# Decode attention with a parallel MLP: V in 4 MB transfers of 32 heads, P turned by VectorE, the last rows of w4 behind V

## The chip, the core and the metric

The kernel runs on one core of a Trainium2 chip. The metric is device microseconds of one execution. Before the change the median of three runs is 215.27 us (215.07 to 215.28). Engines are named TensorE (PE in the profile, PEld for its weight loads), VectorE (DVE), ScalarE (ACT), GpSimd (POOL) and SyncE (SP), which issues nearly all transfers.

## The reference

```python
x = A_x                                   # 4 x 1 x 576, bf16
xn = _layernorm(x)
return x + _A_ref(xn, k_cache, v_cache, wq, wo) + _B_ref(xn, w1, w2, w3, w4)

def _A_ref(...):                          # B = 4, 32 query heads, 16 K/V heads, head size 128
    q = x @ wq                            # one position per batch
    k, v = the last W = 2048 rows of each cache of 8192 rows, each K/V head for two query heads
    p = softmax(q k^T * 128 ** -0.5)
    return (p v) @ wo                     # wo: 4096 x 576

def _B_ref(...):                          # 576 -> 576 -> 4608 -> 576
    h = gelu(layernorm(x) @ w1)
    g0..g3 = the four quarters of h, each shifted along the sequence (which has length 1)
    x1 = x + concat(g0..g3) @ w2
    return x1 + gelu(layernorm(x1) @ w3) @ w4
```

K and V of the window are 33.6 MB each in bf16; the weights are some 21 MB. Everything is read from HBM once.

## The kernel before

The work is one stream of transfers and, beside it, four engines' instruction lists. `add(engine, emit, waits, sig, key)` files an instruction under an engine; each list is sorted by `key` and emitted in that order, with a semaphore wait for each name in `waits`. A list is strictly in order: an instruction that waits holds up all behind it. SyncE's list holds the transfers: wq, w1, w2, w3, w4 in two parts (24 rows and 12 rows per partition), sixteen of K, sixteen of V, five of wo.

**K.** Chunk `c` of K is one batch and four heads (`CH`), 2 MB: partition p holds 64 rows of 128 values, 16 KB in one piece (`kv_src`). There are four slots (`kslot`); K4 and later wait until TensorE has turned the chunk that held the slot (`T`, L496). VectorE and ScalarE copy the turned blocks (L480, L479), and TensorE multiplies them with the padded queries into scores that stay in PSUM (L503).

**Softmax and P.** After the last scores VectorE takes the maximum (L509), ScalarE the exponentials (L513). P has to be turned so that keys lie on partitions. For that VectorE makes four masked copies of each quarter (`dve_mask`, L521), TensorE gathers them by 16 products (`pe_PT`, L530), ScalarE copies, TensorE applies a permutation (L541), ScalarE copies again (L543).

**V.** V comes in the same 2 MB chunks into five slots (`vslot`), the sixteenth into a slot of K. V0 to V4 wait until w4 has been used (`MO1`), V5 and later for the product of the chunk five before (`PV`). For a chunk VectorE spreads P over 32 columns per group of four rows (`dve_pad`, L559: 512 elements per partition); TensorE makes 16 products of 32 columns of P by 512 columns of V, four side by side in column tiles (L567); VectorE masks the useful blocks and sums them (L585, L588); TensorE folds partitions (L573); VectorE scales (L591). Fifteen chunks run in a hardware loop of three turns of five, the last outside it, with idle products ahead of it and of the last fold (`IDLE`).

**The end.** The result is turned (L601 to L603, `ORT`) and multiplied with wo's 32 rows per partition (L386), which come in pieces of 12, 10, 7, 2 and 1 rows (`WO_ROWS`) into three of K's slots once K has been turned. The MLP's sum, kept in `t1f`, is added to the same accumulator (`pe_t1f`, L610). Two copies and two small transfers end the program.

Of the kernel before, what the change touches and what calls it, by code (L numbers as in the profile page):

```python
# [12 lines left out]
NKT = 16  # L13
# [3 lines left out]
NVS = 5  # L17
ACT_EVAC = (1, 4, 7)
WO_ROWS = (12, 10, 7, 2, 1)
IDLE = {NKT - 2: 5, NKT - 1: 5}  # L20
# [14 lines left out]
def bass_parallel_sum__sliding_block_cached__mixer_s_mlp__decode_kernel(  # L35
# [23 lines left out]
    CH = [(b, gq) for gq in range(4) for b in range(B)]  # L59
    x2 = A_x.rearrange("b s d -> (b s) d")  # L60
# [3 lines left out]
    with ExitStack() as ctx:  # L64
# [12 lines left out]
        vslot = lambda c: vring[:, c % NVS * UE:(c % NVS + 1) * UE] if c < NC - 1 else kslot(0)  # L77
# [6 lines left out]
        w4t = vring[:, 4 * F:4 * F + W4R * D].rearrange("p (r n) -> p r n", r=W4R)  # L84
        assert 4 * F + W4R * D <= 5 * UE
        wot = kring[:, UE:UE + 32 * D].rearrange("p (r n) -> p r n", r=32)
        assert 32 * D <= 3 * UE
# [13 lines left out]
        P4 = cut(4 * NU * 512).rearrange("p (q t u i) -> p q t u i", q=4, t=16, u=NU)  # L101
        PTx = cut(4 * 512).rearrange("p (q x) -> p q x", q=4)
        PTpad = cut(NVS * NT * 2 * NU).rearrange("p (s t u e) -> p s t u e", s=NVS, t=NT, u=NU)
        tmp = [cut(2 * 512).bitcast(FP32).rearrange("p (t d) -> p t d", t=4) for _ in range(2)]
        assert _o <= NKT * 1024
        PTv = PT_t[:].rearrange("p (t c e) -> p t c e", t=NT, c=NC)

        acc = sb("acc", [128, NVS, 128], FP32)
# [16 lines left out]
        q_sb = acc[:].rearrange("p a b -> p (a b)").bitcast(BF16)[:, 0:1024].rearrange("p (k x) -> p k x", k=2)  # L125
# [5 lines left out]
        permT_bf = sb("permT_bf", [128, 128], BF16)  # L131
        ident_f = sb("ident_f", [128, 128], FP32)
        ones_f = sb("ones_f", [128, 128], FP32)
        mask4 = sb("mask4", [128, NU], FP32)
        maskd = sb("maskd", [128, 4], FP32)
        sel_f = sb("sel_f", [128, 32], FP32)
        sel_bf = sb("sel_bf", [128, 32], BF16)
        sel8 = sb("sel8", [128, 2 * NU], FP32)
        mU = sb("mU", [128, NU], FP32)
        mU_bf = sb("mU_bf", [128, NU, 2], BF16)  # L140
# [19 lines left out]
        PTps = [ps[:, 4 + k, :].rearrange("p (t x) -> p t x", t=16) for k in range(4)]  # L160
        OTps = [ps[:, 4, 8 * k:8 * k + 8] for k in range(NVS)]
        PVb = [0, 1, 2, 3, 6]
        rinvps = ps[:, 5, 0:128]
        ORps = ps[:, 6, 0:128]
# [18 lines left out]
        for k in range(NVS):  # L183
            for nm in ("PD", "FF", "AA", "OO"):
                S[nm, k] = sem(f"{nm}{k}")
# [31 lines left out]
        for c in range(NC):  # L217
            k, i = c % NVS, c // NVS
            ev_val[f"PV{c}"] = ("PV", c + 1)
            ev_val[f"fold{c}"] = ("FO", c + 2)  # L220
            ev_val[f"pad{c}"] = (("PD", k), i + 1)
            ev_val[f"F{c}"] = (("FF", k), i + 2)
            ev_val[f"A{c}"] = (("AA", k), i + 1 + (k == NVS - 1))
            ev_val[f"O{c}"] = (("OO", k), i + 1 + (k >= NVS - 2))
# [25 lines left out]
        P(lambda e: e.memset(acc[:, NVS - 1, :], 0.0), key=-88, inc=(("AA", NVS - 1), 1))  # L250
        for nm, k in [("FF", k) for k in range(NVS)] + [("OO", NVS - 2), ("OO", NVS - 1)]:
            P(lambda e, nm=nm, k=k: e.sem_inc(S[nm, k], 1), key=-87)


        def mask_of(t, tag, view, axis=AX.X):
            add("dve", lambda e: e.tensor_reduce(out=t[:], in_=view, axis=axis, op=ALU.add), waits=["ident_f"], sig=tag, key=-8)
        mask_of(mask4, "mask4", ident_f[:].rearrange("p (u x) -> p u x", u=NU))
        mask_of(maskd, "maskd", ident_f[:].rearrange("p (j t y) -> p t j y", j=4, t=4), AX.XY)
        mask_of(sel_f, "sel_f", ident_f[:].rearrange("p (u x) -> p x u", u=NU))
        mask_of(sel8, "sel8", ident_f[:].rearrange("p (k x) -> p x k", x=2 * NU))  # L260
        add("dve", lambda e: e.tensor_copy(out=sel_bf[:], in_=sel_f[:]), waits=["sel_f"], sig="sel_bf", key=-7.9)
        mask_of(mU, "mU", ident_f[:].rearrange("p (i u) -> p u i", u=NU))
        for x in range(2):
            add("dve", lambda e, x=x: e.tensor_copy(out=mU_bf[:, :, x], in_=mU[:]), waits=["mU"], sig=f"mU_bf{x}", key=-7.8)
# [10 lines left out]
        ev_w4 = [add_dma([(w4t[:, W4P[k]:W4P[k + 1], :], w4s[:, W4P[k]:W4P[k + 1], :])], ("w4", k), (), -45 + k)  # L275
# [5 lines left out]

        t_done = lambda c: f"T{NBLK * c + NBLK - 1}"
        ev_v = []
# [3 lines left out]
        for c in range(NC):  # L287
# [174 lines left out]
        def pe_MO(k):  # L462
            def f(e):
                ins = None
                for t in range(W4P[k], W4P[k + 1]):
                    for h in range(2):
                        ins = acc_mm(e, h, h2T_sb[:, t, :], w4t[:, t, HALF * h:HALF * (h + 1)], stop=(t == W4R - 1))
                return ins
            return f
        for k in range(2):  # L470
            add("pe", pe_MO(k), waits=[ev_w4[k], "h2T", "t1acc"], sig=f"MO{k}", key=-10 + k)
        add("dve", lambda e: e.tensor_copy(out=t1f[0:B, :], in_=ACC[0]), waits=["MO1"], sig="t1f0", key=-4)
        add("act", lambda e: e.activation(out=t1f[32:32 + B, :], in_=ACC[1], func=ACTF.Copy), waits=["MO1"], sig="t1f1", key=-4)
# [43 lines left out]
        def dve_mask(q):  # L517
            def f(e):
                ins = None
                for u in range(NU):  # L520
                    ins = e.tensor_scalar(out=P4[:, q, :, u, :], in0=P_sb[:, q, :].rearrange("p (t i) -> p t i", t=16),  # L521
                                          scalar1=mask4[:, u:u + 1], scalar2=None, op0=ALU.mult)
                return ins
            return f

        def pe_PT(q):
            def f(e):
                ins = None
                for t in range(16):
                    ins = e.matmul(PTps[q][:, t, :], lhsT=P4[:, q, t].rearrange("p u i -> p (u i)"), rhs=sel_bf[:],  # L530
                                   start=True, stop=True, skip_group_check=True)
                return ins
            return f
        for q in range(4):
            k0 = KS + 0.2 + 0.1 * q
            add("dve", dve_mask(q), waits=[f"exp{q}", "mask4"], sig=f"P4_{q}", key=k0)
            add("pe2", pe_PT(q), waits=[f"P4_{q}"] + (["sel_bf"] + [f"E{NB - 1 - k}" for k in range(4)] if q == 0 else []),
                sig=f"PTp{q}", key=k0)
            add("act", lambda e, q=q: e.activation(out=PTx[:, q, :], in_=ps[:, 4 + q, :], func=ACTF.Copy),  # L539
                waits=[f"PTp{q}"], sig=f"PTx{q}", key=k0 + 0.05)  # L540
            add("pe2", lambda e, q=q: e.matmul(ps[:, q, :], lhsT=permT_bf[:], rhs=PTx[:, q, :], start=True, stop=True),  # L541
                waits=[f"PTx{q}", "permT_bf"], sig=f"PTy{q}", key=k0 + 0.11)
            add("act", lambda e, q=q: e.activation(out=PT_t[:, 512 * q:512 * (q + 1)], in_=ps[:, q, :], func=ACTF.Copy),  # L543
                waits=[f"PTy{q}"], sig=f"PT{q}", key=k0 + 0.16)
# [5 lines left out]
            waits=["diag", "ones_f", "PT3"], sig="rinvp", key=KV + 0.5)  # L550
        add("dve", lambda e: e.tensor_copy(out=rinvB[:].rearrange("p (c u e) -> p c u e", u=NU, e=2),
                                           in_=rinvps.rearrange("p (u c e) -> p c u e", u=NU, e=2)),
            waits=["rinvp"], sig="rinvB", key=KV + 1.5)


        def dve_pad(c):
            b, gq = CH[c]
            cc = 4 * b + gq
            return lambda e: e.tensor_tensor(out=PTpad[:, c % NVS],  # L559
                                             in0=PTv[:, :, cc, :].unsqueeze(2).to_broadcast([128, NT, NU, 2]),  # L560
                                             in1=mU_bf[:].unsqueeze(1).to_broadcast([128, NT, NU, 2]), op=ALU.mult)

        def emit_PV(e, k, v):
            ins = None
            for g in range(NT // 4):
                j = g % 4
# [8 lines left out]
        def pe_idle(n):  # L575
            def f(e):
                for _ in range(n):
                    e.matmul(ps[:, 5, :], lhsT=zeros_bf[:, 0:128], rhs=zeros_bf[:, :], start=True, stop=True)
# [155 lines left out]
```

## Time and profile before

| | |
|---|---|
| median of three runs | 215.27 us |
| the profiled execution, and its span | 215.12 us, 213.9 us |
| busy: TensorE, its loads, VectorE, ScalarE, GpSimd | 151.6, 96.9, 116.8, 64.3, 12.7 us |
| mean granted clock of TensorE | 0.83 |
| bytes through the DMA engines | 88.6 MB, 414 GB/s over the span |
| first K transposes, last scores done | 48.7 us, 129.3 us |
| first and last product with V | 140.4 us, 200.6 us |
| last product with wo ends | 212.0 us |

The span is what the profiler saw of the program; the time of the execution is 1.2 us longer. A row of the time line gives start, duration, engine, line, operation and operands, and in brackets how long the engine was idle before it and what ended that.

### The profile page before, as it was taken

The page shows a single profiled execution, that of the slowest core. Times are in us where ns is not written, and L with a number is a line of the kernel's source. Part 1 is how long each engine was busy: PE and PEld are TensorE (multiplying, and loading weights), DVE is VectorE, ACT ScalarE, POOL GpSimd, SP SyncE. Part 2 cuts the span into 40 slices and gives each one's busy share as a digit, 9 for nine tenths or more (in the row PEclk, how much of TensorE's full clock was granted, in tenths as well). Part 3 has the DMA queues.
Part 4 walks back from the last instruction along what each step waited for, and adds up shares of the span by engine and source line. Part 5 has one row for each costly group of instructions (what it writes and reads, how often), then busy time and mean ns, then how long its engine had stood idle before and what let it go on. Part 6 is the DMA issues. An engine that isn't in the chain of part 4 may idle for free.

```text
span 213.9 us, 4528 instructions
## 1 busy us (share of the span) xinstructions
PE 151.6 (71%) x1984; PEld 96.9 (45%) x1987; DVE 116.8 (55%) x240; ACT 64.3 (30%) x78; POOL 12.7 (6%) x20
## 2 busy tenths in 40 slices
PE   2038478578999999999999971788444455555964
PEld 0013126337878877888887860434111122212332
DVE  4962720015767776667677666759934333334520
ACT  2001032003666666556666665810000000000000
POOL 8950000000000000000000000000000000000000
PEclk9999958889999999999999999557855555555699
DMA  7999989999999999999999999999999999999993
GB/s 277 411 385 494 427 376 440 429 417 420 435 429 420 423 438 426 423 426 438 427 420 429 435 426 420 434 429 417 429 435 423 426 432 435 423 426 432 426 400 122
DMA packets 6802, 88.64 MB, mean 414 GB/s; under 512 B 764, under 2 KB 1160, under 8 KB 1928
## 3 DMA queue, kind: packets, MB, share of 16 engines
q1 hardware_dynamic: 6776, 88.50, 97.7%
q8 instruction: 7, 0.11, 0.2%
q14 instruction: 3, 0.02, 0.0%
q10 hardware_dynamic: 16, 0.01, 0.0%
HBM read 88.49 MB, written 0.00 MB: 414 GB/s over the span
## 4 chain that ended last, share of the span: by engine, by line
DMA 68%; PE 17%; DVE 9%; ACT 3%; issue 1%; SPq 1%
DMA kring<-in_A_k_cache_dram 41%; DMA kring<-in_A_wo_dram 16%; DMA vring<-in_A_v_cache_dram 10%; PE ps L496 7%; DVE xn_bf L312 4%; PE ps L567 3%; PE ps L503 2%; PE ps L358 2%; SPq L202 1%; DVE rmax L509 1%; DVE ktb L521 1%; ACT ktb L539 1%; ACT PT L543 1%; DMA x_sb<-in_A_x_dram 1%; PE ps L386 1%
## 5 line engine op out<-in xcount | busy, mean ns | idle before, releaser
L480 DVE COPY ktb<-ps 128x1024 bf16<-128x1024 bf16 x80 | 53.8, 690 | 24.7 <-PE ps L496 24.2
L496 PE MATMUL ps<-perm_bf,kring 128*128 128x128 bf16 x1024 | 62.6, 219 | 3.0 <-DMA kring<-in_A_k_cache_dram 2.1
L496 PEld LDWEIGHTS ps<-perm_bf,kring 128*128 128x128 bf16 x1024 | 57.2, 98 | 12.6 <-issue 9.8
L479 ACT ACTIVATE ktb<-ps 128x1024 bf16<-128x1024 bf16 x48 | 49.2, 1024 | 31.6 <-PE ps L496 30.8
L567 PE MATMUL ps<-vring,ktb 128*32 128x512 bf16 x240 | 25.8, 575 | 23.2 <-DMA vring<-in_A_v_cache_dram 23.2
L585 DVE TENSOR_TENSOR ktb<-ps,maskd 128x512 f32<-128x512 f32 x16 | 11.0, 690 | 29.6 <-PE ps L567 29.5
L629 ACT ACTIVATE out_sb<-ps 4x288 bf16<-4x288 f32 x1 | 0.4, 402 | 72.4 <-PE ps L386 72.4
L567 PEld LDWEIGHTS ps<-vring,ktb 128*32 128x32 bf16 x240 | 7.1, 121 | 30.9 <-issue 27.3
L503 PE MATMUL ps<-ktb,Qs 128*32 128x512 bf16 x272 | 17.8, 382 | 1.2 <-ACT ktb L479 1.2
L588 DVE TENSOR_REDUCE acc<-ktb 128x128 f32<-128x512 f32 x16 | 16.4, 1028 | 0.5
L573 PEld LDWEIGHTS ps<-sel,acc 128*128 128x128 f32 x34 | 7.3, 268 | 14.6 <-issue 8.8
L573 PE MATMUL ps<-sel,acc 128*128 128x8 f32 x34 | 8.8, 331 | 2.5 <-DVE OTn L591 2.5
L503 PEld LDWEIGHTS ps<-ktb,Qs 128*32 128x32 bf16 x272 | 5.8, 95 | 6.7 <-DVE ktb L480 1.4
L322 PE MATMUL ps<-ident_bf,xn_bf 4*128 4x4 bf16 x8 | 0.6, 170 | 11.4 <-DVE xnT L339 8.9
L386 PE MATMUL ps<-vring,h2T_sb 128*4 128x288 bf16 x72 | 6.4, 348 | 2.5 <-DMA vring<-in_B_w_dram 2.5
L559 DVE TENSOR_TENSOR ktb<-PT,mU_bf 128x512 bf16<-128x512 bf16 x16 | 6.6, 416 | 2.1 <-ACT PT L543 2.1
L312 DVE TENSOR_SCALAR xn_bf<-xn_bf,mv,rstd 4x576 bf16<-4x576 bf16 x1 | 7.4, 7430 | 0.0
L245 POOL MEMSET ktb<- 128x8192 bf16 x1 | 6.9, 6925 | 0.0
L530 PE MATMUL ps<-sel_bf,ktb 128*128 128x32 bf16 x64 | 2.4, 189 | 5.5 <-DVE ktb L521 5.5
L386 PE MATMUL ps<-kring,ORT 128*4 128x288 bf16 x64 | 4.4, 286 | 2.4 <-DMA kring<-in_A_wo_dram 1.8
L322 PEld LDWEIGHTS ps<-ident_bf,xn_bf 4*128 4x128 bf16 x8 | 0.4, 112 | 12.3 <-DVE ragsrc L315 9.0
L386 PEld LDWEIGHTS ps<-vring,h2T_sb 128*4 128x4 bf16 x72 | 3.6, 100 | 5.1 <-DMA vring<-in_B_w_dram 2.7
(117 smaller groups left out, 96.4 us busy)
## 6 DMA issues: line engine op xcount, KB each, us to landing
kring<-in_A_k_cache_dram SPq DMA_DIRECT2D x16, 2048.0 KB, 14.7
vring<-in_A_v_cache_dram SPq DMA_DIRECT2D x15, 2048.0 KB, 22.4
vring<-in_B_w_dram SPq DMA_DIRECT2D x1, 4608.0 KB, 24.9
kring<-in_A_wq_dram SPq DMA_DIRECT2D x1, 4096.0 KB, 12.4
vring<-in_B_w_dram SPq DMA_DIRECT2D x1, 3456.0 KB, 34.7
kring<-in_A_v_cache_dram SPq DMA_DIRECT2D x1, 2048.0 KB, 26.7
ktb<-in_B_w_dram SPq DMA_DIRECT2D x3, 576.0 KB, 14.5
vring<-in_B_w_dram SPq DMA_DIRECT2D x1, 1728.0 KB, 38.3
```

What stands on the lines that cost most here:

```text
L245: P(lambda e: e.memset(ktb[:, NKT // 2 * 1024:NKT * 1024], 0.0), key=-92, inc=(("E", LB - 2), 1))
L312: add("dve", lambda e: e.tensor_scalar(out=dst[:], in0=src[:], scalar1=mv[:, idx, 0:1], scalar2=rstd[:, idx:idx + 1], op0=ALU.subtract, op ...
L386: return e.matmul(ACC[h], lhsT=lhsT, rhs=rhs, start=start, stop=stop, tile_position=(0, 32 * h), skip_group_check=True)
L479: return "act", lambda e: e.activation(out=ktbuf[:, n % NKT], in_=tb[n % 4], func=ACTF.Copy)
L480: return "dve", lambda e: e.tensor_copy(out=ktbuf[:, n % NKT], in_=tb[n % 4])
L496: ins = e.transpose(tb[j % 4][:, t, :], kslot_t(k)[:, 8 * kb + t, :], perm_bf[:])
L503: ins = e.matmul(Sps[32 * u:32 * u + 32, q, :].rearrange("p (t i) -> p t i", t=16), lhsT=Qs[:, k, 32 * u:32 * u + 32], rhs=ktgrp[:, (4 * k ...
L559: return lambda e: e.tensor_tensor(out=PTpad[:, c % NVS], in0=PTv[:, :, cc, :].unsqueeze(2).to_broadcast([128, NT, NU, 2]), in1=mU_bf[:].u ...
L567: ins = e.matmul(ps[32 * j:32 * j + 32, PVb[k], :], lhsT=PTpad[:, k, 4 * g:4 * g + 4].rearrange("p t u e -> p (t u e)"), rhs=v[:, 512 * g: ...
L573: e.matmul(OTps[k], lhsT=acc[:, k, :], rhs=sel8[:], start=True, stop=True, skip_group_check=True).then_inc(S["FO"], 1)
L585: add("dve", lambda e, c=c: e.tensor_tensor(out=tmp[c % 2], in0=ps[:, PVb[c % NVS], :].rearrange("p (t d) -> p t d", t=4), in1=maskd[:].un ...
L588: add("dve", lambda e, c=c: e.tensor_reduce(out=acc[:, c % NVS, :], in_=tmp[c % 2].rearrange("p t d -> p d t"), axis=AX.X, op=ALU.add), wa ...
```

## The change

V is read in eight transfers of 4 MB, each of a pair of batches (32 heads) by a quarter of the window. Partition 4h + i holds 128 rows of head h: 32 KB in one piece (`v_src`). The eighth is issued in two halves of 64 rows. Four slots: two in V's buffer, two in K's. V0 and V1 wait for `MO0`, V2 and V3 until K's slots are turned (chunks 13 and 15), V4 to V7 for the second product of the chunk four before.

P is turned by VectorE (32 x 32 blocks, one instruction per quarter); TensorE then gathers each quarter by 16 products of 256 columns with 0/1 matrices (`pick_bf`, built by GpSimd at the start), and VectorE and ScalarE each copy two quarters. P is padded to 64 columns per row, for all 32 heads: 4096 elements per partition and half chunk. A product is 128 columns of P (two rows) by 256 columns of V, without column tiles; 32 products make a half, all accumulate into one bank over four chunks, and mask, sum and fold come once per pair of batches. Four idle products (`V_IDLE`) stand ahead of every fourth chunk.

w4's last 12 rows are transferred behind V, and their products stand in the end, half ahead of the last fold and half behind it, with two idle products (`O_IDLE`) after the result is turned. wo goes to V's buffer in pieces of 13, 10, 5, 3 and 1 rows; the first 28 rows wait for the second product of V's chunk 4, the last four for that of chunk 5.

```diff
-NVS = 5
+NVS = 4
+NPAIR = 2
 ACT_EVAC = (1, 4, 7)
-WO_ROWS = (12, 10, 7, 2, 1)
-IDLE = {NKT - 2: 5, NKT - 1: 5}
+WO_ROWS = (13, 10, 5, 3, 1)
+WOA = 28
+V_IDLE = 4
+O_IDLE = 2
...
+    VCH = [(bp, qt) for bp in range(NPAIR) for qt in range(NVS)]
+    NCV, NTV = len(VCH), 2 * NT
+    NH = NTV // 2
+    NX = 2 * Hkv
-        vslot = lambda c: vring[:, c % NVS * UE:(c % NVS + 1) * UE] if c < NC - 1 else kslot(0)
+        vslot = lambda k: (vring, vring, kring, kring)[k][:, k % 2 * 2 * UE:(k % 2 + 1) * 2 * UE]
...
+        wo_at = lambda a: a * D if a < WOA else 2 * UE + (a - WOA) * D
+        wot = lambda a, n: vring[:, wo_at(a):wo_at(a) + n * D].rearrange("p (r n) -> p r n", r=n)
...
-        ev_w4 = [add_dma([(w4t[:, W4P[k]:W4P[k + 1], :], w4s[:, W4P[k]:W4P[k + 1], :])], ("w4", k), (), -45 + k)
+        ev_w4 = [add_dma([(w4t[k], w4s[:, W4P[k]:W4P[k + 1], :])], ("w4", k), ["PTp3"] if k else (), KS + NCV if k else -45)
...
+        def v_src(c, t0, t1):
+            bp, qt = VCH[c]
+            k0 = Sk - W + 4 * NTV * qt
+            return A_v_cache[2 * bp:2 * bp + 2, :, k0:k0 + 4 * NTV, :].rearrange(
+                "b h (i t) d -> (b h) i (t d)", t=NTV)[:, :, Dh * t0:Dh * t1]
-        for c in range(NC):
-            w = [t_done(NC - N_CB)] if c == NC - 1 else [f"PV{c - NVS}"] if c >= NVS else ["MO1"]
-            ev_v.append(add_dma([(vslot(c), kv_src(A_v_cache, c))], ("v", c % NVS if c < NC - 1 else NVS), w, KS + c))
+        for c in range(NCV):
+            w = [f"PV{2 * (c - NVS) + 1}"] if c >= NVS else [t_done(NC - N_CB + 2 * c - 3)] if c >= 2 else ["MO0"]
+            for n, (u0, u1) in enumerate([(0, NH), (NH, NTV)] if c == NCV - 1 else [(0, NTV)]):
+                add_dma([(vslot(c % NVS)[:, Dh * u0:Dh * u1], v_src(c, u0, u1))], ("v", c % NVS, n), w, KS + c + 0.1 * n)
-            ev_wo.append(add_dma([(wot[:, a:a + rc, :], wos[:, a:a + rc, :])], ("wo", n), [t_done(NC - 1)], KS + NC + n))
+            ev_wo.append(add_dma([(wot(a, rc), wos[:, a:a + rc, :])], ("wo", n), [f"PV{2 * (NCV - NVS + (a >= WOA)) + 1}"], KS + NC + n))
...
+        PTx_v = PTx.rearrange("p q (t a b g e) -> p (q t) a b g e", t=16, a=NPAIR, b=2, g=4)
+
-                for u in range(NU):
-                    ins = e.tensor_scalar(out=P4[:, q, :, u, :], in0=P_sb[:, q, :].rearrange("p (t i) -> p t i", t=16),
-                                          scalar1=mask4[:, u:u + 1], scalar2=None, op0=ALU.mult)
+                for ih in range(2):
+                    for gl in range(2):
+                        for j in range(4):
+                            ins = e.matmul(ps[32 * j:32 * j + 32, 4 + qt, 256 * ih:256 * (ih + 1)].rearrange("p (t a e) -> p t a e", a=NPAIR, e=2),
+                                           lhsT=pick_bf[:, 2 * qt + ih, gl, :], rhs=PTx_v[:, :, :, j // 2, 2 * (j % 2) + gl, :],
+                                           start=(gl == 0), stop=(gl == 1), tile_position=(0, 32 * j), skip_group_check=True)
...
+            add("dve", lambda e, q=q: e.transpose(PTx[:, q, :], P_sb[:, q, :]), waits=[f"exp{q}"], sig=f"PTx{q}", key=KS + 0.2 + 0.1 * q)
+        for qt in range(4):
+            k0 = KS + 0.9 + 0.1 * qt
+            add("pe2", pe_PT(qt), waits=[f"PTx{q}" for q in range(4)] + (["pick217"] + [f"E{NB - 1 - k}" for k in range(4)] if qt == 0 else []),
+                sig=f"PTp{qt}", key=k0)
+            if qt % 2 == 1:
+                add("dve", lambda e, qt=qt: e.tensor_copy(out=PT_t[:, 512 * qt:512 * (qt + 1)], in_=ps[:, 4 + qt, :]),
+                    waits=[f"PTp{qt}"], sig=f"PT{qt}", key=k0)
+            else:
+                add("act", lambda e, qt=qt: e.activation(out=PT_t[:, 512 * qt:512 * (qt + 1)], in_=ps[:, 4 + qt, :], func=ACTF.Copy),
+                    waits=[f"PTp{qt}"], sig=f"PT{qt}", key=k0)
...
+        def dve_pad(n):
+            c, h = n // 2, n % 2
+            bp, qt = VCH[c]
+            return lambda e: e.tensor_tensor(out=PTpad[:, n % 4],
+                                             in0=PTv[:, qt, NH * h:NH * (h + 1), bp, :].unsqueeze(2).to_broadcast([128, NH, NX, 2]),
+                                             in1=mH_bf[:].unsqueeze(1).to_broadcast([128, NH, NX, 2]), op=ALU.mult)
+
+        def emit_PV(e, k, h):
             ins = None
-            for g in range(NT // 4):
-                j = g % 4
-                ins = e.matmul(ps[32 * j:32 * j + 32, PVb[k], :], lhsT=PTpad[:, k, 4 * g:4 * g + 4].rearrange("p t u e -> p (t u e)"),
-                               rhs=v[:, 512 * g:512 * (g + 1)], start=(g < 4), stop=(g >= 12),
-                               tile_position=(0, 32 * j), skip_group_check=True)
+            for g in range(NH // 2):
+                t = NH * h + 2 * g
+                ins = e.matmul(ps[:, 0, 0:256], lhsT=PTpad[:, 2 * (k % 2) + h, 2 * g:2 * g + 2].rearrange("p t h e -> p (t h e)"),
+                               rhs=vslot(k)[:, Dh * t:Dh * (t + 2)], start=(k == 0 and t == 0), stop=(k == NVS - 1 and t == NTV - 2),
+                               skip_group_check=True)
             ins.then_inc(S["PV"], 1)
...
+        for n in range(2 * NCV):
+            w = [f"PV{n - 4}"] if n >= 4 else ["mH_bf1", f"PT{n // 2}"]
+            add("dve", dve_pad(n), waits=w + ([f"PT{n // 2}"] if n in (4, 6) else []), key=KV + n - 3, inc=(("PD", n % (2 * NVS)), 1))
+        for bp in range(NPAIR):
+            k0 = KV + 2 * NVS * (bp + 1) - 0.5
+            add("dve", lambda e: e.tensor_scalar(out=tmp[:], in0=ps[:, 0, 128:256], scalar1=maskd[:, 1:2], scalar2=None, op0=ALU.mult),
+                waits=[f"PV{2 * NVS * (bp + 1) - 1}", "maskd"], sig=f"F{bp}", key=k0)
+            add("dve", lambda e: e.scalar_tensor_tensor(out=acc[:], in0=ps[:, 0, 0:128], scalar=maskd[:, 0:1], in1=tmp[:],
+                                                        op0=ALU.mult, op1=ALU.add), waits=[f"F{bp}"], key=k0 + 0.1, inc=("AA", 1))
+            cs = slice(2 * NX * bp, 2 * NX * (bp + 1))
+            add("dve", lambda e, cs=cs: e.tensor_tensor(out=OTn[:, cs], in0=OTps, in1=rinvB[:, cs], op=ALU.mult),
+                waits=["rinvB", f"fold{bp}"], sig=f"O{bp}", key=k0 + (3 if bp == 0 else 0.2))
+        add("pe3", lambda e: emit_fold(e), waits=[f"A{NPAIR - 1}", "O0"], key=KE - 2)
+
...
+        add("pe3", pe_t1f, waits=["t1f0", "t1f1", "PT3"], sig="t1in", key=KE - 4)
+        W4M = (W4P[1] + W4R) // 2
+        add("pe3", pe_MO(1, W4P[1], W4M), waits=[ev_w4[1], "h2T"], key=KE - 3)
+        add("pe3", pe_MO(1, W4M, W4R), key=KE - 1)
+        add("pe3", pe_idle(O_IDLE), key=KE + 0.25)
...
-        with nc.Fori(0, (NC - 1) // NVS, engines=[PE]) as it:
+        e.wait_ge(S["dve"], resolve("mH_bf1")[1])
+        with nc.Fori(0, NPAIR, engines=[PE]) as it:
             turn = e.snap(it + 1)
             landed = e.snap(16 * it + 16)
             for k in range(NVS):
-                e.wait_ge(S["PD", k], turn)
-                e.wait_ge(S["FF", k], turn)
-                e.wait_ge(S["v", k], landed)
-                emit_PV(e, k, vslot(k))
-                e.wait_ge(S["AA", (k - 1) % NVS], turn)
-                e.wait_ge(S["OO", (k - 2) % NVS], turn)
-                emit_fold(e, (k - 1) % NVS)
+                for h in range(2):
+                    e.wait_ge(S["PD", 2 * k + h], turn)
+                    if k == 0 and h == 0:
+                        e.wait_ge(S["AA"], turn)
+                    if h == 0 or k == NVS - 1:
+                        e.wait_ge(S["v", k, h], landed)
+                    if k == NVS - 1 and h == 0:
+                        pe_idle(V_IDLE)(e)
+                    emit_PV(e, k, h)
+                if k == 0:
+                    emit_fold(e)
```

More of the change, by code (lines that the diff above doesn't have):

```diff
@@ L83, in bass_parallel_sum__sliding_block_cached__mixer_s_mlp__decode_kernel @@
         w3main = vring[:, 0:4 * F].rearrange("p (r n) -> p r n", r=4)
[L84 to L87, printed above, removed]
+        w4t = [vring[:, a:a + n * D].rearrange("p (r n) -> p r n", r=n) for a, n in ((4 * F, W4P[1]), (4 * UE, W4R - W4P[1]))]
+        assert 4 * F + W4P[1] * D <= 4 * UE and (W4R - W4P[1]) * D + 1024 <= UE
+        assert WOA * D <= 2 * UE
+        wo_at = lambda a: a * D if a < WOA else 2 * UE + (a - WOA) * D
+        wot = lambda a, n: vring[:, wo_at(a):wo_at(a) + n * D].rearrange("p (r n) -> p r n", r=n)
         _o = 0
@@ L100, in bass_parallel_sum__sliding_block_cached__mixer_s_mlp__decode_kernel @@
         _o = 0
[L101 to L104, printed above, removed]
+        PTx = vring[:, 4 * UE:4 * UE + 4 * 512].rearrange("p (q x) -> p q x", q=4)
+        PTpad = cut(4 * NH * 2 * NX).rearrange("p (s t h e) -> p s t h e", s=4, t=NH, h=NX)
         assert _o <= NKT * 1024
-        PTv = PT_t[:].rearrange("p (t c e) -> p t c e", t=NT, c=NC)
-        acc = sb("acc", [128, NVS, 128], FP32)
+        PTv = PT_t[:].rearrange("p (q t b e) -> p q t b e", q=NVS, t=NTV, b=NPAIR)
+        acc = sb("acc", [128, 128], FP32)
+        tmp = sb("tmp", [128, 128], FP32)
         x_sb = sb("x_sb", [B, D], BF16)
@@ L257, in bass_parallel_sum__sliding_block_cached__mixer_s_mlp__decode_kernel @@
[L257 to L262, printed above, removed]
+        P(lambda e: e.memset(acc[:], 0.0), key=-88, inc=("AA", 1))
@@ new lines, in bass_parallel_sum__sliding_block_cached__mixer_s_mlp__decode_kernel @@
+        P(lambda e: e.sem_inc(S["v", NVS - 1, 1], 16), key=-87)
+        P(lambda e: e.memset(pick_bf[:], 0.0), sig="pick0", key=-86)
+        for gl in range(2):
+            pick_v = pick_bf[:, :, gl, 16 * gl:16 * gl + 16]
+            P(lambda e, v=pick_v: e.memset(v, 1.0), waits=["pick0"], sig=f"pick1{gl}", key=-85 + 0.1 * gl)
+        for gl in range(2):
+            for x in range(2 * NVS):
+                v = pick_bf[:, x, gl, 16 * gl:16 * gl + 16].rearrange("p (u r) -> p u r", u=NU)
+                P(lambda e, v=v, x=x: e.affine_select(out=v, in_=v, compare_op=ALU.is_equal, fill=0.0, base=-(8 * (x // 2) + x % 2),
+                                                      pattern=[[-NI, NU], [-2, 4]], channel_multiplier=1),
+                  waits=["pick11"], sig=f"pick2{gl}{x}", key=-84 + 0.1 * (8 * gl + x))
@@ L263, in bass_parallel_sum__sliding_block_cached__mixer_s_mlp__decode_kernel, with mask_of @@
+        def mask_of(t, tag, view):
+            add("dve", lambda e: e.tensor_reduce(out=t[:], in_=view, axis=AX.X, op=ALU.add), waits=["ident_f"], sig=tag, key=-8)
+        mask_of(maskd, "maskd", ident_f[:].rearrange("p (t y) -> p t y", t=2))
+        mask_of(sel64, "sel64", ident_f[:].rearrange("p (k x) -> p x k", x=2 * NX))
+        mask_of(mH, "mH", ident_f[:].rearrange("p (h i) -> p h i", h=NX))
         for x in range(2):
-            add("dve", lambda e, x=x: e.tensor_copy(out=mU_bf[:, :, x], in_=mU[:]), waits=["mU"], sig=f"mU_bf{x}", key=-7.8)
+            add("dve", lambda e, x=x: e.tensor_copy(out=mH_bf[:, :, x], in_=mH[:]), waits=["mH"], sig=f"mH_bf{x}", key=-7.8)
@@ new lines, in bass_parallel_sum__sliding_block_cached__mixer_s_mlp__decode_kernel @@
+        for bp in range(NPAIR):
+            k0 = KV + 2 * NVS * (bp + 1) - 0.5
[6 more added lines that the diff above has]
+                waits=["rinvB", f"fold{bp}"], sig=f"O{bp}", key=k0 + (3 if bp == 0 else 0.2))
```

121 lines of the change are left out of this document (31 added, 90 removed).

## The prediction

> **What bounds the kernel now.** I read the page first. Its DMA strip and queue table:
>
> ```profile
> DMA  7999989999999999999999999999999999999993
> q1 hardware_dynamic: 6776, 88.50, 97.7%
> ```
>
> The 16 DMA engines are busy from the second slice to the last but one. All 88.5 MB stand in one queue, and nothing is fetched twice. Is a queue ever empty? I cut the span into stages (busy time of each engine, granted clock, DMA share, GB/s):
>
> ```profile
> 46.00:126.00 80.00, 77.03 (x1280) 62.15 (x1275) 54.59 (x95) 47.73 (x48) 0.00 (x0) 1.00 1.01 428
> 160.00:200.00 40.00, 20.98 (x148) 8.71 (x149) 17.30 (x34) 0.00 (x0) 0.00 (x0) 0.50 1.01 428
> ```
>
> The K stage and the V stage move the same 428 GB/s, though TensorE works 96% of one and 52% of the other. So transfers set the pace. The time line of the V stage shows who waits for whom, and SyncE's rows how early the transfers are asked for:
>
> ```profile
> 108.13 65.64 SPq L202 DMA_DIRECT2D vring<-in_A_v_cache_dram  x15
> 166.41 1.90 PE L567 MATMUL ps<-vring,ktb 128*32 128x512 bf16 x16 [2.47 <-DMA vring<-in_A_v_cache_dram]
> 170.09 0.41 DVE L559 TENSOR_TENSOR ktb<-PT,mU_bf 128x512 bf16<-128x512 bf16 x1
> 171.30 1.90 PE L567 MATMUL ps<-vring,ktb 128*32 128x512 bf16 x16 [2.46 <-DMA vring<-in_A_v_cache_dram]
> ```
>
> Each 2 MB of V lands 4.89 us after the one before; TensorE has finished and waits 2.5 us. V is asked for a median 22.4 us before it lands: four to five transfers are always queued. Last the end, from the chain of waits:
>
> ```profile
> 175.56 34.97 DMA kring<-in_A_wo_dram
> 210.58 1.44 PE ps L386 x20
> 212.01 0.44 DVE out_sb L628
> ```
>
> So the time is: a head of 2.3 us, one unbroken stream, and a tail. Removing TensorE, VectorE or ScalarE work can't shorten it; only fewer nanoseconds per byte, or a gap in the stream, can move it.
>
> **The change, part by part.**
>
> *Larger runs.* Seven of the eight 4 MB transfers go as 32,768 B pieces instead of 16,384 B; the last, split in two, keeps 16,384 B. An engine carries 8 pieces of each transfer: 112 pieces become 56. What does a piece cost beyond its bytes? Two windows of the DMA view, 17.7 to 28.1 us (w3, 36,864 B pieces) and 156 to 196 us (V, 16,384 B):
>
> ```profile
> q1 hardware_dynamic: 157, 4.28, 95.5%
> q1 hardware_dynamic: 1174, 17.12, 100.5%
> ```
>
> 4.28 MB / (0.955 x 16 x 10.4 us) = 26.9 B/ns per engine; 17.12 / (1.005 x 16 x 40) = 26.6. The two rates differ by 1.2%; solved for a fixed part per piece that is 0.433 ps/B over (1/16,384 - 1/36,864), some 13 ns. The trace's own packet records give less: medians of 613 ns at 16,384 B, 1365.5 at 36,864, 159 at 4,096, so 8 to 11 ns. I take 10, nearest to the like-sized pieces: 56 x 10 = 0.56 us. Seven fewer transfers save as many 9 ns end marks: 0.06. Together 0.6 us, bounds 0.5 (8 ns) to 0.8 (13 ns). Below nothing is possible if the new addresses read slower (rival).
>
> *w4's 12 rows* (1728 KB, 4.1 us at 428 GB/s) move from before K to behind V: the sum in the queue is unchanged, 0. K lands 4.1 us earlier, the first at 48.7 - 4.1 = 44.6. TensorE ends the 24 rows at 44.4, then clears banks (0.8) and waits for t1f (0.5): it starts K about 1.3 us late. Cover: four K slots, 14.7 us from issue to landing. The 24 matmuls (1.64 us) and two idle ones move to the tail, ahead of and between the fold and OR. V's end to wo's first 13 rows: 4.1 + 4.5 us. After w4 lands, half the matmuls 0.8, fold 0.36, O 0.17, turn 0.31, OR 0.23, copy 0.44, the other half 0.8: 3.1 against 4.5 us for the 13 rows. 0; uncovered, 3.1.
>
> *SyncE's order.* V2 and V3 wait for the turning of K13 and K15, V4 to V7 for PV1, 3, 5, 7; w4's rest and wo stand behind them. Does the stream run dry at V4? K ends at 122.2 - 4.1 = 118.1; V0 to V3 feed it 38.8 us, to 156.9. Chain to PV1: scores end 125.2 (129.3 - 4.1), maximum and exp to 130.6. VectorE turns of 128x512: the only row is 128x128 at 0.31, so 0.31 to 1.24; I take 0.7 (L585's 512 elements, 0.69), the last behind its exp: 131.4. P's gather: 16 matmuls of 256 columns, four abreast: half of L503's 0.98 to half of L567's 1.90, so 0.5 to 0.95. ScalarE copy 0.6. Pad: 4096 elements against 512 in 0.41: 1.9 (if 0.15 of it is fixed, as in L591's row) to 3.3; I take 2.5. First product at 136 to 137. One half is 32 matmuls of 256 columns: L578's 0.25 per 512 at the high clock gives 4.0, L567's 0.42 per 512 in the clock of 0.50 gives 6.8. PV1 ends at 145 to 151, six us or more ahead of need. Later: 8 us per 4 MB at the high clock against 9.7 of transfer. VectorE: 16 pads of 2.5 are 40 us within 78. 0.
>
> *The rest.* 16 masks (4.3 us), four PTy products, four ScalarE copies, 15 folds, 32 mask-and-reduce steps go: all hidden, 0. GpSimd gets some 19 small instructions (its selects take 0.2 to 0.5): 4 to 9 us after 13.4 us, beside early VectorE work; K's 14.7 us of queue cover it. wo in 13, 10, 5, 3, 1: the last piece is one row as before; 0, or up to 0.5 if the last groups run at the lower clock.
>
> Sum: 215.12 of the profiled execution - 0.6 = 214.5; it lies 0.15 below the median of 215.27, so 214.7 against that.
>
> **The rivals.** About 0.2% (0.43 us) is what a measurement of this kernel can tell from no change.
>
> *The gain is lost at the end (same).* A landing counts when the slowest of 16 engines is done, and they drift: over 206 to 214 us the DMA strip thins out,
>
> ```profile
> DMA  9997969799699699484445442100000000000000
> ```
>
> so over the last 2.4 us a growing half of the engines has finished. 0.2 to 0.5 us in the tail gives 214.9 to 215.2. For: the gain is hardly above the bound. Against: the last pieces are alike.
>
> *A code block hits the slowest engine (slower).* The V loop holds 256 products and as many weight loads where 80 of each stood: some 20 KB more. Code comes as 16 KB blocks (q8: seven, 0.11 MB) through these engines; in the packet records an engine that carried one ends later transfers 1.5 us behind. Seven blocks went to different engines, which speaks against a second on one; if it happens, 214.7 + 1.5 = 216.2. It decides as soon as one engine carries two.
>
> *Heads at a large stride read slower (slower).* Engines formerly read 32 KB apart; now, if each takes eight neighbouring partitions, 4 MB apart at the same step. No row has that stride. The slowest rows of big pieces are wq's 32,768 B at the start, mean 1295 ns against a median of 1215: 6.6% of V's 78.2 us is 5.2, so 219.9. The Trainium skill (DMA: Bandwidth & Descriptors, "Latency and other measured facts") warns of this: row pitches of 2 MiB cut a copy from 207 to 164 GB/s. By it V would take 20 us more, 235. Its 512 KiB pitch, eight rows to an engine, is also 4 MiB between engines and ran at full rate; no run here shows either.
>
> *TensorE stays at half clock (slower).* In 160 to 200 us it was granted 0.50. At that, 4 MB take 13.6 us against 9.7 and V lasts 8 x 13.6 from 137: about 246, with wo's last products 250. It decides below a clock of about 0.7. For: these rows. Against: the K stage, busy 96%, had 1.00, and late products would be just as dense. The Trainium skill (TensorE: Matmul & The Clock Gate, Part 1) says some 3.4 us of steady work lifts the clock; a half of 6.8 us would, and the rival falls.
>
> **The numbers.** Forecast (stream shorter by 0.5 to 0.8, nothing else) 0.49; lost at the end 0.19; code block 0.18; stride 0.09; half clock 0.05. Faster 0.49, same 0.19, slower 0.32. The likeliest is 214.7; its own range is 214.3 to 214.9. For 8 in 10 the range must take in the code block and may leave out stride and clock (0.14): 214.2 to 216.6.
>
> **What would show it.** Right: V's 4 MB land 9.70 to 9.72 us apart instead of 9.78; DMA share stays 1.0 until about 210.9; V's first product before 138; TensorE's waits in V end on DMA; K's first landing near 44.6. Wrong: a DMA share under 1 between 150 and 160 (V4 late); V rows further apart than 9.8 (stride); products without waits (clock); wo's last row beyond 211.6 with V on time (code block or tail).

## The result, and the profile after

The changed kernel takes 214.85 us (median; 214.31 to 215.82) against 215.27: ratio 0.9977, 95% interval [0.9967, 0.9987]. That is 0.4 to 0.5 us faster; 214.7 was predicted. The profiled execution also took 214.85 us, its span 213.5 (before 213.9). A second set of runs of the same kernel gave 214.79, ratio 0.9976 [0.996, 0.9991].

The DMA strip and the queue table of the page (columns: packets, MB, share of the 16 engines' span):

```profile
DMA  7999989999999999999999999999999999999992
q1 hardware_dynamic: 5768, 88.49, 97.5%
q8 instruction: 8, 0.13, 0.2%
q14 instruction: 3, 0.02, 0.0%
```

The same bytes in 1008 fewer packets: 63 an engine, the 56 pieces and 7 end marks of the forecast. Still no slice is empty: the kernel is one unbroken stream, as before. The windows of the K and the V stage (busy time of TensorE, its loads, VectorE, ScalarE and GpSimd, granted clock, DMA share, GB/s):

```profile
46.00:118.00 72.00, 70.89 (x1206) 59.01 (x1205) 51.28 (x90) 43.79 (x45) 0.00 (x0) 1.00 1.01 428
160.00:200.00 40.00, 33.61 (x302) 29.28 (x301) 14.52 (x10) 0.00 (x0) 0.00 (x0) 1.00 0.99 425
```

In the V stage TensorE is busy 84% of the time instead of 52%, and its granted clock is 1.00 instead of 0.50; it costs nothing, because the queue still sets the pace. The time line of V, with the first product, the issue that decides whether the stream runs dry, and the steady state:

```profile
136.40 7.16 PE L576 MATMUL ps<-vring,ktb 128*128 128x256 bf16 x64 [0.80 <-DVE ktb L568]
143.59 7.69 SPq L205 DMA_DIRECT2D vring<-in_A_v_cache_dram  x2
...
176.66 7.15 PE L576 MATMUL ps<-vring,ktb 128*128 128x256 bf16 x64 [2.48 <-DMA vring<-in_A_v_cache_dram]
186.37 7.15 PE L576 MATMUL ps<-kring,ktb 128*128 128x256 bf16 x64 [2.56 <-DMA kring<-in_A_v_cache_dram]
194.21 7.15 PE L576 MATMUL ps<-kring,ktb 128*128 128x256 bf16 x64
```

Two successive starts that a landing released are 186.37 - 176.66 = 9.71 us apart, where before it was twice 4.89. The last row has no wait in its bracket: V7's products start because V6's and the idle products behind them have ended, not because V7 has landed. The end, from the time line:

```profile
204.75 1.76 PE L399 MATMUL ps<-vring,ORT 128*4 128x288 bf16 x26 [0.19 <-DVE ORT L605]
208.07 1.39 PE L399 MATMUL ps<-vring,ORT 128*4 128x288 bf16 x20 [1.55 <-DMA vring<-in_A_wo_dram]
```

wo's first group starts when the turned result is ready (VectorE's `ORT`), its second waits for a transfer: up to 204.75 TensorE is late, behind it the queue is.

The trace's packet records (start, duration and size of every piece) tell where the 0.4 us came from, by the time at which the slowest engine ends each transfer. Times from these records are given 0.43 us later than the DMA view has them, so that the last end mark of a transfer falls on the landing that the waits show. Up to the end of w4's first part it is 0.11 less; sixteen chunks of K take 78.33 instead of 78.53 us, V 78.22 instead of 78.32, and the remainder 0.06 less. V's term looks small because six of the 4 MB steps took 9.70 to 9.72 us, and one, from 146.90 to 157.07, took 10.17. The DMA view of 146 to 158 us has what came in that step:

```profile
q1 hardware_dynamic: 177, 5.08, 98.9%
q8 instruction: 1, 0.02, 0.6%
q14 instruction: 1, 0.01, 0.2%
```

A 16 KB and an 8 KB block of code came, at 148.6 and 148.8 us. After them the slowest of the 16 engines ends 2.21 us behind the fastest, instead of 1.88, up to wo's first rows. The pieces of one engine follow each other without a pause, so an engine can be followed through the records. The 16 KB block took 1.08 us and the piece behind it 1.71 instead of 1.21; the engine, one of the first, ended 1.55 us later and still wasn't the last. The 8 KB block took 0.33 us and the piece behind it 1.88; its engine had been 0.50 us ahead of the last one, fell back by 0.97 and became the last. These are the 0.46 us.

### The profile page after: what moved, and what is told of

Read it like the earlier page. It is cut to its first block, busy times and chain, and to the rows that moved or that the text cites. A ratio compares the mean times of both kernels' runs of the same rounds, so it can differ in the third digit from the quotient of the medians.

```text
span 213.5 us, 4894 instructions
## 1 busy us (share of the span) xinstructions
PE 170.0 (80%) x2207; PEld 131.6 (62%) x2211; DVE 119.2 (56%) x185; ACT 59.8 (28%) x72; POOL 16.3 (8%) x39
## 4 chain that ended last, share of the span: by engine, by line
DMA 47%; PE 44%; DVE 4%; SPq 2%; issue 1%; ACT 1%
PE ps L508 23%; DMA vring<-in_B_w_dram 16%; DMA vring<-in_A_wo_dram 13%; DMA vring<-in_A_v_cache_dram 12%; PE ps L576 10%; DMA kring<-in_A_k_cache_dram 7%; PE ps L515 6%; PE ps L399 3%; SPq L205 2%; DVE vring L543 1%; DVE rmax L521 1%; DVE ktb L568 1%; PE ps L537 1%; ACT ktb L491 0%; PE ps L345 0%
## 5 line engine op out<-in xcount | busy, mean ns | idle before, releaser
L508 PE MATMUL ps<-perm_bf,kring 128*128 128x128 bf16 x1024 | 60.6, 219 | 1.1 <-issue 1.1
L491 ACT ACTIVATE ktb<-ps 128x1024 bf16<-128x1024 bf16 x48 | 47.7, 1023 | 30.2 <-PE ps L508 30.1
L568 DVE TENSOR_TENSOR ktb<-PT,mH_bf 128x4096 bf16<-128x4096 bf16 x16 | 36.2, 2287 | 13.3 <-PE ps L576 13.3
L576 PE MATMUL ps<-vring,ktb 128*128 128x256 bf16 x256 | 28.6, 273 | 4.6 <-DMA vring<-in_A_v_cache_dram 3.8
L576 PE MATMUL ps<-kring,ktb 128*128 128x256 bf16 x256 | 28.6, 273 | 2.6 <-DMA kring<-in_A_v_cache_dram 2.6
L576 PEld LDWEIGHTS ps<-vring,ktb 128*128 128x128 bf16 x256 | 24.8, 98 | 7.9 <-issue 3.6
L576 PEld LDWEIGHTS ps<-kring,ktb 128*128 128x128 bf16 x256 | 25.0, 98 | 6.1 <-issue 2.8
L537 PE MATMUL ps<-vring,pick_bf 128*32 128x256 bf16 x64 | 3.9, 411 | 6.4 <-DVE rinv L555 6.4
L537 PEld LDWEIGHTS ps<-vring,pick_bf 128*32 128x32 bf16 x64 | 2.1, 121 | 8.2 <-DVE rinv L555 6.9
L399 PE MATMUL ps<-vring,ORT 128*4 128x288 bf16 x64 | 4.6, 286 | 2.4 <-DMA vring<-in_A_wo_dram 2.2
```

The source lines that it names most:

```text
L399: return e.matmul(ACC[h], lhsT=lhsT, rhs=rhs, start=start, stop=stop, tile_position=(0, 32 * h), skip_group_check=True)
L491: return "act", lambda e: e.activation(out=ktbuf[:, n % NKT], in_=tb[n % 4], func=ACTF.Copy)
L508: ins = e.transpose(tb[j % 4][:, t, :], kslot_t(k)[:, 8 * kb + t, :], perm_bf[:])
L537: ins = e.matmul(ps[32 * j:32 * j + 32, 4 + qt, 256 * ih:256 * (ih + 1)].rearrange("p (t a e) -> p t a e", a=NPAIR, e=2), lhsT=pick_bf[:, ...
L568: return lambda e: e.tensor_tensor(out=PTpad[:, n % 4], in0=PTv[:, qt, NH * h:NH * (h + 1), bp, :].unsqueeze(2).to_broadcast([128, NH, NX, ...
L576: ins = e.matmul(ps[:, 0, 0:256], lhsT=PTpad[:, 2 * (k % 2) + h, 2 * g:2 * g + 2].rearrange("p t h e -> p (t h e)"), rhs=vslot(k)[:, Dh * ...
```

## The experiments

Each kernel is the changed one with a single edit, unless another is named, and is compared with the kernel before on the same chip. "After" stands for 214.85 and 214.79; differences are taken from 214.85. The kernel before had medians of 215.27 to 215.38 on the chips used.

**1. Same change, V in 16 KB pieces.** If the larger pieces are the gain, it goes; what is left is what the remaining parts do together.

```diff
-for n, (u0, u1) in enumerate([(0, NH), (NH, NTV)] if c == NCV - 1 else [(0, NTV)]):
+for n, (u0, u1) in enumerate([(0, NH), (NH, NTV)]):
...
-if h == 0 or k == NVS - 1:
+if True:                       # each half is waited for
     e.wait_ge(S["v", k, h], landed)
```

> The changed kernel with each of V's eight 4 MB transfers issued as two halves of 16,384 B pieces, as only the last one is in the change. Same addresses, same order, same slots; 56 more pieces and 7 more end marks per engine. Theory (a piece costs about 10 ns beyond its bytes): 0.6 us slower than the changed kernel, so level with the kernel before, 215.2 to 215.5, and 4 MB of V land 9.78 us apart instead of 9.71. Rival (the size of a piece does not matter and the gain came from the move of w4 or the smaller chain): no difference, 214.8 to 214.9.

215.40 us, ratio 1.0008 [0.9988, 1.0028]: no difference from before, 0.55 us above after. The page's queue table has the packets of before again:

```profile
q1 hardware_dynamic: 6776, 88.50, 97.5%
```

So the order of transfers, VectorE's turn, the new products and the moved rows of w4 come to nothing together within this interval (0.4 us either way), and the pieces are the gain. Without the end marks, (0.55 - 0.06) / 56 is 8.7 ns a piece. The traced execution took 216.44: behind a 16 KB block of code at 165.3 us one step of V took 0.83 us more, and wo's last row landed at 212.65. Its undisturbed steps took 9.78 to 9.80 us for 4 MB.

**2. V in 8 KB pieces.** The cost of a piece on a longer lever: 184 pieces more per engine.

```diff
+for n, (u0, u1) in enumerate([(x * NH // 2, (x + 1) * NH // 2) for x in range(4)]):
```

> The changed kernel with each 4 MB of V issued in four transfers of 8,192 B pieces: 256 pieces of V per engine instead of 72, 23 more end marks. Theory (10 ns a piece): 184 x 10 ns + 0.2 = 2.0 us slower than the changed kernel, about 216.9; at 8 ns 1.7, at 13 ns 2.6. 4 MB land 9.95 us apart. Rival (pieces are free): no difference.

216.47 us, ratio 1.0052 [1.0034, 1.0069], 1.62 above after. Less 0.2 for the end marks, (1.62 - 0.2) / 184 is 7.7 ns a piece. The queue table:

```profile
q1 hardware_dynamic: 9080, 88.50, 97.9%
```

Three piece sizes lie in the order of their number, at 8 to 9 ns each. The intervals of the medians alone would allow 4 to 11 ns; the packet records are sharper. In them 4 MB of V take 9.94 us here, 9.79 before, 9.71 after: less the end marks that are 8 to 9 ns a piece as well, and the forecast's 10 was too much.

**3. w4's last 12 rows ahead of K again.** They are transferred and multiplied where they were before; the end has neither.

```diff
-... ["PTp3"] if k else (), KS + NCV if k else -45)
+... (), -45 + k)
...
+add("pe", pe_MO(1, W4P[1], W4R), waits=[ev_w4[1]], sig="MO0", key=-9)
...
-add("pe3", pe_MO(1, W4P[1], W4M), waits=[ev_w4[1], "h2T"], key=KE - 3)
-add("pe3", pe_MO(1, W4M, W4R), key=KE - 1)
```

> The changed kernel with w4's last 12 rows back ahead of K and their products back ahead of the first scores. Theory (the sum in the queue is what counts): no difference from the changed kernel, 214.6 to 215.1; K's first landing moves back to 48.7 us, and the chain after V's last product ends some 1.5 us before or after wo's first 13 rows without reaching the end. Rival (the change gains by having 4.1 us more transfer behind V to cover the last fold): 0.5 us or more slower than the changed kernel.

215.54 us, ratio 1.0031 [1.0, 1.0061]: 0.7 slower than after by the medians; the move is not neutral. Four executions took 215.42 to 215.55 and two 217.2 and 217.3; the traced one took 217.31. The strip, and the time line of the end:

```profile
DMA  7999999999999999999999999999999999999970
```

```profile
198.46 7.15 PE L577 MATMUL ps<-kring,ktb 128*128 128x256 bf16 x64
...
208.39 5.76 PE L399 MATMUL ps<-vring,ORT 128*4 128x288 bf16 x64 [0.20 <-DVE ORT L606]
```

V's last byte lands at 200.2 and wo's last at 211.3. TensorE does V7's products until 205.5, folds and turns until 208.39, and then does all 64 products with wo in one block, without a wait for a transfer. It ends at 214.15, 2.9 us behind wo's last byte, where after's last group follows its transfer. In this execution the granted clock was 0.50 during most of them (columns as in the table of the stages above):

```profile
208.58:211.99 3.41, 3.41 (x32) 1.97 (x30) 0.00 (x0) 0.00 (x0) 0.00 (x0) 0.50 0.31 121
```

The 64 products took 5.76 us; at the pace of experiment 9 (56 in 3.88 us) they would take 4.4. So the order of events is read from this trace, the price of 0.7 us from the medians; no trace shows an execution at the median. With 4 MB transfers and 7.15 us of products for each, the work behind V's last byte has become longer than wo's transfers; w4's 4.15 us, put behind V, cover it.

**4. Four more code blocks during V.** ScalarE is idle in V; it gets 1024 waits that are already met, which are only code.

```diff
+def act_code(e):
+    for _ in range(1024):
+        e.wait_ge(S["pool"], 1)
+add("act", act_code, key=KV)
```

> The changed kernel with 1024 waits on a semaphore that has long been raised, put into ScalarE's list after its last copy of P, where ScalarE is idle to the end: about 64 KB more code, four or more blocks of 16 KB, no work. Theory (code comes through the same 16 engines; each block sets one engine back by up to 1.5 us, and the end waits for the slowest): q8 shows some 12 blocks instead of 8, the engines end further apart, and the time is 0 to 1.5 us longer depending on which engines carry them, 215.0 to 216.3. Rival (code is free beside 88 MB): no difference in time, and V's landings stay 9.71 us apart.

216.24 us, ratio 1.004 [1.0024, 1.0056], 1.4 above after. The waits became 512 instructions and came as four blocks of 8 KB in q14; q8 didn't grow, though I had expected it to:

```profile
q8 instruction: 8, 0.13, 0.2%
q14 instruction: 7, 0.06, 0.1%
```

Apart from q14 the transfers are those of after. In the packet records a block keeps its engine for 0.31 us, and behind those at 167.7 and 178.1 us the slowest engine falls back by 0.3 and 0.7 us against the fastest: the spread goes from 2.33 to 2.64 to 3.33 us and stays, and these two steps of V take 10.03 and 10.40 us instead of 9.71. Followed by its pieces, one engine carried all four blocks. Each time the piece behind the block took 1.59 us instead of 1.21, so that the engine lost 0.7 us a block. It had been among the first, and the first two blocks cost nothing; the third made it the last, and the fourth counted in full.

**5. The same blocks in the kernel before.** What they cost without the change.

```diff
+add("act", act_code, key=KV)   # act_code as in 4, in the kernel before
```

> The kernel before with the same 1024 waits on ScalarE as in the run with code blocks, after its last copy of P. Theory (any block on the 16 engines sets one of them back, and the end waits for the slowest): 0.5 to 1.5 us slower than the kernel before, as the changed kernel was 1.4 us slower with it. Rival (the changed kernel is hit by something else that ScalarE's waits do, such as its last copy starting late): no difference here, and ScalarE's last copy not later behind its product.

216.86 us, ratio 1.0076 [1.0059, 1.0094], 1.6 slower; q14 has the same seven packets:

```profile
q8 instruction: 7, 0.11, 0.2%
q14 instruction: 7, 0.06, 0.1%
```

The spread grows from 2.1 to 3.7 us. Two steps of 2 MB take 5.57 us instead of 4.89, behind the blocks at 170.7 and 180.6 us, and the pieces behind the blocks take 0.99 instead of 0.61; here too one engine carried all four. The price belongs to the shared engines, not to the changed kernel.

**6. The changed kernel once more,** with no edit.

> The changed kernel once more, unaltered, beside the kernel before and the next three on one chip: 214.6 to 215.0. A second trace of it shows whether a code block that arrives during V again sets the slowest engine back: in the first one 4 MB of V landed 9.71 us apart six times and 10.17 us once, right after the blocks at 148.7 us.

214.79 us. The packet records have V's steps at 9.71 us again, and the same exception: 147.08 to 157.21, 10.13 us, with code blocks at 148.9 and 149.0 and a spread that grows from 2.02 to 2.45. It came in two executions, then, and in experiment 9's too (10.04 us); experiment 7 is without it. One thing differs from the first trace. At 176.78 us, behind a pause of 2.46 us, the 64 products of one chunk took 8.81 us instead of 7.15. The row of the time line, and a window inside it (columns as above):

```profile
176.78 8.81 PE L576 MATMUL ps<-vring,ktb 128*128 128x256 bf16 x64 [2.46 <-DMA vring<-in_A_v_cache_dram]
177.40:180.70 3.30, 3.30 (x18) 2.24 (x16) 0.00 (x0) 0.00 (x0) 0.00 (x0) 0.50 1.04 447
```

The granted clock of the window was 0.50. Still, 8.81 is under the 9.71 of a transfer, and the time is the same.

**7. V's first product some 8 us later.** 40 idle products stand ahead of the first one.

```diff
+add("pe2", lambda e: pe_idle(40)(e), waits=["PT2"], key=KV + 0.6)
```

> The changed kernel with 40 idle products of 512 columns on TensorE between the gather of P and the first product with V: every product with V starts some 8 to 9 us later. Theory (transfers are asked for early enough: V4 is issued at 143.6 us and the queue lasts to about 155): no difference, 214.6 to 215.1, TensorE catches up within V. Rival (V's products or P's turn are on the path): up to 8 us slower.

214.70 us, ratio 0.9977 [0.9961, 0.9992]: nothing lost. The time line:

```profile
144.65 7.15 PE L577 MATMUL ps<-vring,ktb 128*128 128x256 bf16 x64
151.83 7.69 SPq L205 DMA_DIRECT2D vring<-in_A_v_cache_dram  x2
```

V4 is asked for 8.24 us later and still lands in its place in the queue: the seven steps of V are 9.71 us each. Here the code blocks came 4 to 7 us later, the engines were already 2.2 us apart when V began, and no step of V is longer than the others.

**8. V's first product 19 us later.** 90 idle products instead of 40.

```diff
+add("pe2", lambda e: pe_idle(90)(e), waits=["PT2"], key=KV + 0.6)
```

> The same with 90 idle products, about 19 us. Theory (11 us of margin, then every microsecond counts): V4 is issued at some 162 us, the queue is empty for 6 to 8 us, and the kernel takes 221 to 223 us; the DMA strip shows the hole after 155 us. Rival (the margin lies elsewhere, for example in slots freed by later products): no difference, or the full 19 us.

225.24 us, ratio 1.0458 [1.0441, 1.0475], 10.4 above after, more than expected. The time line, and the DMA strip of 140 to 180 us (1 us a digit):

```profile
155.39 7.15 PE L577 MATMUL ps<-vring,ktb 128*128 128x256 bf16 x64
162.57 7.69 SPq L205 DMA_DIRECT2D vring<-in_A_v_cache_dram  x2
```

```profile
DMA  7999996999989951000000029699998999979999
```

The engines finish V3 at 154.7 to 156.9 and carry nothing until about 164, though V4 was issued at 162.57: 1.3 us lie between the issue and the first piece on the DMA view's own times, 1.8 us on those used here, which I had left out. So the margin after is 154.9 - 143.6 - 1.8 = 9.5 us, and 19 - 9.5 leaves 9.5 of the 10.4 that were lost. Together with experiment 7 this brackets it: 8 us are free, 19 cost 10.

**9. V's last 4 MB whole.** The candidate for more: eight pieces fewer, one wait. The idle products (`V_IDLE`) are left out too.

```diff
-... [(0, NH), (NH, NTV)] if c == NCV - 1 else [(0, NTV)]
+... [(0, NTV)]
...
-V_IDLE = 4
+V_IDLE = 0
```

> The last 4 MB of V is issued whole instead of in two halves, eight pieces of 32 KB to an engine for eight more of 16 KB, and TensorE waits for it once. Saved at the queue: 8 pieces by the 8 to 9 ns that the halves measured, some 0.07 us. Theory (w4's 4.15 us and wo's last rows behind V cover what TensorE does after V's last byte): V7's 64 products begin at its landing, near 196, or when V6's end near 193.3, whichever is later, and so end near 203.3 instead of 201.3, two microseconds later; wo's first products move from 204.7 to about 206.8, of which the wait for wo's last rows at 208 to 211 takes it back. 214.6 to 215.0, no difference from the changed kernel. Rival: the cover is used up, and the two microseconds show at the end, 216 to 217; or TensorE, idle for 2.7 us ahead of V7, runs its products at half the clock, 13.6 us, and ends at 210 with wo's products behind it, 220 or more.

214.66 us, ratio 0.9978 [0.9966, 0.9991]: no difference from after; 0.07 us is less than can be told. The time line of the end shows the cover almost used up:

```profile
196.12 7.15 PE L575 MATMUL ps<-kring,ktb 128*128 128x256 bf16 x64 [1.11 <-DMA kring<-in_A_v_cache_dram]
...
206.66 3.88 PE L398 MATMUL ps<-vring,ORT 128*4 128x288 bf16 x56 [0.19 <-DVE ORT L604]
210.84 0.66 PE L398 MATMUL ps<-vring,ORT 128*4 128x288 bf16 x8 [0.29 <-DMA vring<-in_A_wo_dram]
```

V7 starts 1.9 us later than after, so do the products with wo, and only the last eight still wait for their transfer, 0.29 us. No version clearly faster than the changed kernel came out of these runs.

## Why the prediction was right

**Larger runs.** The mechanism held and the term was sized a little high: 0.5 to 0.55 us instead of 0.6. A piece costs 8 to 9 ns beyond its bytes, not 10; that is the lower end of the packet records (8 to 11 ns), and the 13 ns of the two windows was too much. Experiment 1 shows that this term is the whole gain, within its interval. In the profiled execution the 0.5 us is split oddly: six of V's steps are 0.07 us shorter, and the one with code blocks gives nearly all of that back, while the head and K, whose pieces didn't change, are 0.3 us shorter. That the stream of this pair still ends 0.46 us earlier is luck: in the one before, a step of K behind a code block took 5.16 us, in the one after none took over 4.93. How far apart the engines are differs between the traced executions, and after's runs lie up to 1.5 us apart; the size of the term rests on the medians and on the undisturbed steps.

**w4's 12 rows.** "0" was right, its working not. TensorE started K at 47.45, 3.1 us behind K's first landing, not 1.3: the 48 products of w4's first part took 5.92 us at a granted clock of 0.50 and ended at 45.42 instead of 44.4, and 2.0 us instead of 1.3 lay between them and K. The chain of waits shows the next 56 us as TensorE's own products back to back, until K's transfers are waited for again at 103.76:

```profile
39.50 5.92 PE ps L399 x48
...
47.45 1.51 PE ps L508 x24
...
103.76 13.99 DMA kring<-in_A_k_cache_dram
```

K's four slots covered it, as the text said. The tail's chain was "3.1 against 4.5 us"; V7's products, which end 5.3 us behind V's last byte, were left out. `ORT` was ready 8.6 us after it (V's last byte at 195.98, the wo row that follows at 204.75), against 4.15 + 4.46 for w4's rows and wo's first 13: no slack at all at that row, and the 1.55 us of waiting at wo's second group is what saved the term. There the "0" was luck: the forecast had 1.4 us of slack, and its chain left out what took it. Experiment 3 shows what the same work costs without w4's rows behind V: 0.7 us.

**SyncE's order.** Turn 0.68 us (0.7 taken), a gather 0.97 (0.5 to 0.95), first product 136.40 (136 to 137), PV1's end 143.56 (145 to 151; the two halves took 7.16 us at a granted clock of 1.00, against 4.0 to 6.8 each in the forecast). The pad is a row of the page:

```profile
L568 DVE TENSOR_TENSOR ktb<-PT,mH_bf 128x4096 bf16<-128x4096 bf16 x16 | 36.2, 2287 | 13.3 <-PE ps L576 13.3
```

2.29 us against 2.5. "Six us or more ahead of need" was some 9, by experiments 7 and 8.

**The rivals.** *Half clock* didn't set the pace: 7.15 us per 4 MB, granted 1.00 throughout V in after's trace. By the Trainium skill's rule on steady work (TensorE: Matmul & The Clock Gate, Part 1) it fell too; in the trace the clock rose to 1.00 at 134.1 us, 2.8 us after the gather's products had begun. It wasn't as far off as that trace has it: behind pauses of 2.2 to 2.6 us the clock fell to 0.50 for 3.4 us in the traces of experiments 4, 6 and 9, and 4 MB took 8.6 to 8.8 us there. *Heads at a large stride* didn't occur: 4 MB in 9.71 us, the larger run's gain in full. The loss that the Trainium skill (DMA: Bandwidth & Descriptors, "Latency and other measured facts") measured at a 2 MiB pitch, 207 to 164 GB/s for copies between HBM tensors, did not show in these transfers into the core, with heads 2 MiB apart and four partitions to a head. *The code block* was real: V has blocks at 136.5, 148.6 and 163.7 us, and the second set V back by 0.46. The forecast's 1.5 us is what the 16 KB block cost its engine (1.55), but that engine had been among the first. The 8 KB block cost its engine 0.97 us; that one had been 1.4 us behind the first already, and so the kernel paid half of it. Experiments 4 and 5 show the price of four blocks on one engine, 1.4 to 1.6 us. *The gain lost at the end* didn't occur: the last row landed at 211.20 instead of 211.65. Against the forecast's own signs, six of V's seven undivided steps and the first product were as said, and K's first landing was at 44.3 (44.6). Of TensorE's eight chunks of V only three waited for a transfer (V4 to V6): V0 waited for VectorE, V1 to V3 were worked off without a wait, since each had landed before TensorE came to it, and V7 had its first half there already.

## What to carry to other kernels

When the queue never empties, ask of a change only what it does to pieces, bytes and code that pass through the engines; price a piece from the packet records of like-sized pieces, since two windows of the DMA view contain other things. When transfers grow, the work behind the last landing grows with them: follow that chain from the last byte with the products in it, and put transfers behind it that nothing waits for early. Measure a cover by using it up, with one run inside it and one beyond.

## What the runs showed of the hardware

Code is not free to a kernel that is bound by transfers. An 8 KB block held one of the 16 engines 0.31 to 0.33 us and a 16 KB block some 1.05, and the piece behind the block took 0.4 to 0.7 us longer than others: a block of 8 KB set its engine back by 0.7 to 1.0 us, one of 16 KB by 1.55. Engines do not share what they fall behind: each carries its own part of every transfer, so a landing comes with the slowest. They ended 1.8 to 2.5 us apart throughout K and V in after's two traces. What a block costs the kernel therefore depends on whom it strikes: nothing on an engine that is further ahead than the block sets it back, its whole price on the last. Four more blocks of 8 KB, which would be 0.08 us if the 16 engines shared them, came to one engine in each kernel and made both 1.4 to 1.6 us slower. Why the piece behind a block takes longer is not settled by these runs.
